# One planner run from a stored table of priorities, and PSUM matmuls tied in order

## The chip, the core and the metric

The kernel runs on one NeuronCore of a Trainium2 chip. The metric is the device time of one execution in microseconds (us), median over runs. The engines are TensorE (PE), ScalarE (ACT), VectorE (DVE), GpSimd (POOL) and SyncE (SP); SP issues all the DMAs of this kernel. Each engine works off its own queue in program order and waits on semaphores for the others.

## The reference

What is computed, cut to what matters (two batches, 8 heads, 768 positions, head size 64; then two feed-forward layers on 1536 tokens, width 512, hidden width 2048):

```python
q_bits = (q @ proj > 0); k_bits = (k @ proj > 0)
mask = q_bucket[:, :, :, None] == k_bucket[:, :, None, :]
scores = where(mask, q @ k.T / sqrt(64), -1e9)
attn = exp(scores - max); attn = attn / (sum(attn) + 1e-9)
x = (attn @ v) as tokens x 512
h = x @ w_in;  x = (h * sigmoid(h)) @ w_out
h = x @ w2_in; x = (h * clip(h + 3, 0, 6) / 6) @ w2_out
```

All inputs and outputs are float32. The kernel keeps the accuracy by splitting each operand into two float16 parts (high and low) and multiplying three of the four combinations.

## The kernel before

**The work.** Batch 0 has four head pairs, batch 1 four more. A pair is prepared (`Pair.prepare`, L715): q and k are loaded (L612), their squares summed on ACT (L382), scaled and split into halves (L388 on ACT, L394 on DVE or POOL), transposed by DMA (L652), hashed (products L665, sums L671, penalties L677), and transposed again with the penalties in the spare columns (L696). `Unit` (L723) then does one pair and one block of two query tiles, in four slots: scores (L749, L750), negated row maximum (L753 on DVE), scale and bias (L755, L758), exponential with row sum (L761 on ACT), and the product with v. In batch 0, blocks 0 and 1, this product is exact: PE transposes (L777), copies (L783) and float32 matmuls (L789). Elsewhere the exponentials are split in two float16 halves (L808 on ACT, L810 on POOL or DVE), transposed by DMA (L813) and multiplied (L803). `finish` (L818) divides and writes the block into X^T by another DMA transpose (L847).

The weights come in chunks (`Weight`, L403): load into one of three stage buffers `st` (L444 on SP), then L446 (ACT), L447 (POOL), L449 and L451 (DVE), square sums, and after all chunks of a group the splits (L388, L394). W1I and W1O are the weights of the first layer, W2I and W2O those of the second.

`mlp1` (L884) does the first layer for one block of 256 tokens: 16 hidden tiles (matmuls called at L876, activation L919, DVE product L921, split L388 and L394), then four output tiles of 48 matmuls each (L933). `mlp2` (L975) does the second layer for groups of 512 or 256 tokens: L876, L1008, L1012, L1014, L1015, L1016, L1021, results scaled (L1037) and stored (L1040).

**What sets the order.** Nothing is issued when this code is reached. Each step is an `op` (L215): one or more `ways` (engine, cost from the fixed formulas of class `Cost`, function), the cells that it reads and writes, and the `take` and `give` of a shared PSUM buffer. Dependences follow from the cells. A step such as L394, L755, L783, L810 or L1037 has two ways, and the planner picks the engine. There are 3171 steps. `Run` (L114) is a list scheduler: it keeps a model time for each engine, and picks again and again the step that can start earliest (`choose`, L190); the rank decides only between steps with the same start:

```python
key = (s, -self.ranks[i], sign * i, e)
```

`Run.start` (L170) also models the DMA queue and the SBUF port that POOL and some DVE steps share, and `Clock` (L81) a TensorE clock with two levels. `Plan.issue` (L255) takes the longest path behind each step (`paths`, L245) as the first ranks, runs the planner forward, runs it backward over the result, takes the ends of the backward run as the next ranks, and does so 24 times (`PASSES`). The best forward run by model time is issued, engine by engine, in its order and with its choice of ways (L264). `follows` (L861) links PE steps by a soft edge, used by `paths` alone.

**PSUM and order.** A group of matmuls that accumulates in one bank is cut into several PE steps: two for each hidden tile (L914 to L917), eight for each output tile of `mlp1` (L940 to L943), 16 for each output tile of `mlp2` (L1030 to L1032). The first matmul of a group carries `start=True`. Before the change no dependence orders the steps of one bank among each other.

Of the kernel before, what the change touches and what calls it, by code (L numbers as in the profile page):

```python
# [2 lines left out]

# [262 lines left out]

# [859 lines left out]
```

## Time and profile before

| | us |
|---|---|
| median of three runs | 746.33 |
| lowest and highest run | 745.91 to 746.54 |
| span of the profiled execution, first to last instruction | 745.7 |
| PE busy in the span | 689.2 |
| ACT busy | 513.1 |
| DVE busy | 507.3 |
| POOL busy | 182.5 |

The profile has no second time for its execution than the span, which ends 0.6 us below the median of the runs. Busy times are unions of the instructions' spans on an engine. A matmul in a stream is shown with its own latency, so the mean of one is longer than the distance between two.

### The profile page before, as it was taken

Reading aid. Unit: us, or ns where it says so; the run is one execution under the profiler, and the core shown is the slowest. Engines: PE = TensorE matmul, PEld = TensorE weight load, DVE = VectorE, ACT = ScalarE, POOL = GpSimd, SP = SyncE. Lnnn points to the kernel's source line nnn. Section 1 sums busy time; section 2 is a strip of 40 time slices with the busy share of each in tenths; the row PEclk is TensorE's granted clock in tenths of the full one; section 3 lists DMA queues with packets and bytes.
Section 4 is the critical chain, followed back from the end, with each engine's and each line's share of the span. In section 5 each row is a group of like instructions: output and inputs, shape, how many; then the busy total and the mean of one; then the engine's idle time right before and its main releaser. Section 6 shows DMA issues by size and latency. Waiting matters only on the chain.

```text
span 745.7 us, 15542 instructions
## 1 busy us (share of the span) xinstructions
PE 689.2 (92%) x6012; PEld 507.9 (68%) x6012; DVE 507.3 (68%) x1157; ACT 513.1 (69%) x1016; POOL 182.5 (24%) x174
## 2 busy tenths in 40 slices
PE   0499989669999999899999999999999999999997
PEld 0288878548778888788888888864445664444564
DVE  5898999899878987887795889843333443333343
ACT  7689999989989987898676888832324334233433
POOL 1011322243656675677422220000000000000000
PEclk9999999859999999999999999999999999999999
DMA  9999465586899999999746450000000000000100
GB/s 263 253 256 251 147 186 170 191 181 139 190 214 207 215 211 194 214 168 177 198 145 220 134 182 2 1 2 0 1 1 30 28 1 29 1 1 0 57 1 29
DMA packets 182474, 91.19 MB, mean 122 GB/s; under 512 B 164992, under 2 KB 172160, under 8 KB 182400
## 3 DMA queue, kind: packets, MB, share of 16 engines
q1 hardware_dynamic: 182400, 90.20, 50.2%
q8 instruction: 47, 0.77, 0.4%
q14 instruction: 27, 0.22, 0.1%
HBM read 44.57 MB, written 3.15 MB: 64 GB/s over the span
## 4 chain that ended last, share of the span: by engine, by line
PE 56%; DMA 13%; ACT 12%; DVE 10%; issue 5%; POOL 2%; SPq 2%; POOLq 0%; ACTq 0%; DVEq 0%
PE h L876 22%; PE s L1021 17%; PE h L933 9%; DMA T<-G 3%; DMA PT<-PN 3%; ACT e L761 3%; ACT sq L382 3%; PE o L789 2%; DVE nm L753 2%; DMA st<-in_moe_w_in_dram 2%; PE s L749 2%; PE s L750 2%; PE o L803 1%; PE h L777 1%; ACT PN L808 1%
## 5 line engine op out<-in xcount | busy, mean ns | idle before, releaser
L1021 PE MATMUL s<-y,G 128*128 128x512 f16 x576 | 134.6, 379 | 0.8 <-ACT w L1037 0.8
L933 PE MATMUL h<-G,w 128*128 128x256 f16 x1152 | 134.1, 273 | 0.1
L810 POOL TENSOR_TENSOR PN<-e,PN 128x768 f16<-128x768 f32 x64 | 107.8, 1687 | 73.5 <-ACT PN L808 55.3
L876 PEld LDWEIGHTS <-w 128*128 128x128 f16 x1152 | 112.0, 99 | 20.0 <-issue 2.7
L933 PEld LDWEIGHTS <-w 128*128 128x128 f16 x1152 | 110.7, 98 | 14.3 <-issue 0.5
L1008 ACT ACTIVATE g<-h,table 128x256 f32<-128x256 f32 x96 | 50.6, 561 | 88.0 <-PE h L876 87.9
L761 ACT ACTIVATE e<-s,nb,sc 128x768 f32<-128x768 f32 x96 | 96.3, 1003 | 3.9 <-DVE nb L758 2.3
L1021 PEld LDWEIGHTS <-G 128*128 128x128 f16 x576 | 56.2, 98 | 62.7 <-issue 1.1
L753 DVE TENSOR_REDUCE nm<-s 128x1 f32<-128x768 f32 x96 | 91.2, 951 | 11.1 <-PE s L750 10.4
L1012 DVE TENSOR_SCALAR g<-g 128x512 f32<-128x512 f32 (+1 forms) x64 | 23.1, 360 | 103.3 <-ACT g L1008 103.3
L876 PEld LDWEIGHTS <-T 128*128 128x128 f16 x576 | 56.4, 98 | 42.1
L447 POOL TENSOR_SCALAR st<-st 128x512 f32<-128x512 f32 x64 | 50.3, 787 | 140.3 <-ACT w L446 59.8
L749 PE MATMUL s<-T 128*128 128x384 f16 x192 | 65.3, 341 | 16.2 <-ACT e L761 16.0
L1015 ACT ACTIVATE G<-g 128x512 f16<-128x512 f32 (+1 forms) x64 | 33.4, 522 | 64.5 <-DVE g L1014 62.8
L876 PE MATMUL h<-X,w 128*128 128x256 f16 x576 | 71.8, 276 | 1.1 <-DVE g L921 1.1
L876 PE MATMUL h<-T,w 128*128 128x256 f16 x576 | 65.1, 272 | 2.5 <-DVE hx L366 1.0
L750 PE MATMUL s<-T 128*128 128x384 f16 x192 | 65.6, 342 | 1.0 <-DMA T<-N 0.8
L1016 DVE TENSOR_TENSOR G<-g,G 128x512 f16<-128x512 f32 (+1 forms) x64 | 35.7, 559 | 41.1 <-ACT G L1015 40.5
L808 ACT ACTIVATE PN<-e 128x768 f16<-128x768 f32 x61 | 51.1, 840 | 6.8 <-DMA PT<-PN 6.5
L876 PE MATMUL h<-X,T 128*128 128x512 f16 (+1 forms) x288 | 50.9, 326 | 0.0
L876 PE MATMUL h<-T,T 128*128 128x512 f16 (+1 forms) x288 | 50.7, 326 | 0.0
L789 PE MATMUL o<-w,PT 128*128 128x64 f32 x384 | 46.2, 271 | 0.2 <-DVE x L838 0.2
(123 smaller groups left out, 1106.4 us busy)
## 6 DMA issues: line engine op xcount, KB each, us to landing
st<-in_moe_w_in_dram SPq DMA_DIRECT2D x32, 512.0 KB, 4.5
st<-in_moe_w_out_dram SPq DMA_DIRECT2D x32, 512.0 KB, 3.5
qk<-in_v_dram SPq DMA_DIRECT2D x8, 384.0 KB, 4.0
out_dram<-w SPq DMA_DIRECT2D x12, 256.0 KB, 2.0
qk<-in_q_dram SPq DMA_DIRECT2D x6, 384.0 KB, 3.6
qk<-in_k_dram SPq DMA_DIRECT2D x6, 384.0 KB, 4.3
w<-in_v_dram SPq DMA_DIRECT2D x2, 768.0 KB, 9.5
T<-T SPq DMA_DIRECT2D x8, 192.0 KB, 3.2
```

What stands on the lines that cost most here:

```text
L447: op((POOL, Cost.pool_ts(512), lambda: nc.gpsimd.tensor_scalar(st.t[:, :, 1].bitcast(F32), st.t[:, :, 1].bitcast(F32), 0.0, 1.0, op0=ALU.m ...
L749: nc.tensor.matmul(o, t.t[:, 0, c, :], t.t[:, 1, ks, :], start=True, stop=False)
L750: nc.tensor.matmul(o, t.t[:, 2, c, :], t.t[:, 3, ks, :], start=False, stop=True)
L753: op((DVE, 0.865, lambda: nc.vector.tensor_reduce(nm.t, ps.t[:, :, :HS], op=ALU.max, axis=AX.XY, negate=True)), [(ps, 0)], [(nm, 0)])
L761: op((ACT, 0.97, lambda: nc.scalar.activation(e.t.rearrange("p (n c) -> p n c", n=2), ps.t[:, :, :HS], AF.Exp, bias=nb.t, scale=sc.t, accu ...
L789: nc.tensor.matmul(po(), pt.t[:, kt, :], vraw.t[:, v0 + a, kt * D : (kt + 1) * D], start=(kt == 0), stop=(kt == T - 1))
L808: op(ways((ACT, Cost.act(S), lambda: nc.scalar.activation(pn.t[:, 0], e.t, AF.Copy)), (DVE, 0.47, lambda: nc.vector.tensor_copy(pn.t[:, 0] ...
L810: op(ways((POOL, Cost.pool_tt(S), lambda: nc.gpsimd.tensor_tensor(pn.t[:, 1], e.t, pn.t[:, 0], op=ALU.subtract)), (DVE, Cost.tt(S), lambda ...
L876: nc.tensor.matmul(ph, W[f, wl, kt, :], XT[b].t[:, kt, ts, xl, :], start=(c == 0), stop=(c == 3 * NK - 1))
L933: nc.tensor.matmul(pf.t[:, :n], W1O[f, wl, slice(m * P, (m + 1) * P)], G.t[:, f, gl], start=(f == 0 and c == 0), stop=(f == NF - 1 and c = ...
L1008: nc.scalar.activation(g.t[:, cs], pf.t[:, cs], AF.Relu, bias=three, scale=a)
L1021: nc.tensor.matmul(acc[m // 2].t[:, m % 2, :DM], gs.t[:, f % 3, gl, m * P : (m + 1) * P], W2O[f, wl], start=(f == 0 and c == 0), stop=(f = ...
```

## The change

`PASSES`, `paths` and the alternation of forward and backward runs are removed. A string `RANKS` is added; unpacked it holds one whole number of 16 bits for each of the 3171 steps, and these are the ranks of a single forward run. `nearest` takes out every dependence that follows from others, before that run. Each PE step on a PSUM bank of the two layers writes a further cell, `(bank, "seq")`, so that the steps of one bank depend on each other in the order in which the code makes them. `Cost`, `Run`, the tiles, the buffers and every instruction's function stay.

```diff
-PASSES = 24
+RANKS = (
...
+)
...
-    def paths(self):
...
+    def ranks(self):
+
+        raw = zlib.decompress(base64.b85decode(RANKS))
+        n = len(raw) // 2
+        assert n == len(self.ops)
+        ranks = [0] * n
+        for i in range(n):
+            ranks[i] = (ranks[i - 1] * (i > 0) + raw[i] + 256 * raw[n + i]) & 0xFFFF
         return ranks
 
+    def nearest(self):
+
+        behind = [0] * len(self.ops)
+        for o in self.ops:
+            o.succ = []
+        for o in self.ops:
+            far = 0
+            for d in o.deps:
+                far |= behind[d.index]
+            behind[o.index] = far
+            for d in o.deps:
+                behind[o.index] |= 1 << d.index
+            o.deps = {d for d in o.deps if not far >> d.index & 1}
+            for d in o.deps:
+                d.succ.append(o)
+
     def issue(self):
 
-
-        best, ranks = None, self.paths()
-        for _ in range(PASSES):
-            run = Run(self.ops, ranks)
-            if best is None or run.time < best.time:
-                best = run
-            ranks = Run(self.ops, run.ends, run.engines).ends
+        self.nearest()
+        best = Run(self.ops, self.ranks())
         for i in best.order:
             next(w[2] for w in self.ops[i].ways if w[0] == best.engines[i])()
...
-                               xt_cells(b, tiles) + W1I.cells(f + i), [(pf, i, h)]))
+                               xt_cells(b, tiles) + W1I.cells(f + i), [(pf, i, h), (pf, "seq")]))
...
-                           gc + W1O.cells(f) + W1O.cells(f + 1), [(pf, f)]))
+                           gc + W1O.cells(f) + W1O.cells(f + 1), [(pf, f), (pf, "seq")]))
...
-                           xt_cells(b, tiles) + W2I.cells(f), [cells[h]]))
+                           xt_cells(b, tiles) + W2I.cells(f), [cells[h], (pf, "seq")]))
...
-                               [(gs, (f - 1) % 3, 0), (gs, (f - 1) % 3, 1)] + W2O.cells(f - 1), [(acc[m // 2], m, f)]))
+                               [(gs, (f - 1) % 3, 0), (gs, (f - 1) % 3, 1)] + W2O.cells(f - 1), [(acc[m // 2], m, f), (acc[m // 2], m, "seq")]))
```

## Rows read from the trace of the kernel before

**Rows 1.** The page: span, then busy time, share and instructions of each engine.

```profile
span 745.7 us, 15542 instructions
PE 689.2 (92%) x6012; PEld 507.9 (68%) x6012; DVE 507.3 (68%) x1157; ACT 513.1 (69%) x1016; POOL 182.5 (24%) x174
```

**Rows 2.** Busy time by stretch: length, engines, granted clock, DMA share, GB/s.

```profile
0.00:41.75 41.75, 14.22 (x100) 10.04 (x101) 29.33 (x85) 28.80 (x52) 4.85 (x15) 1.00 1.01 254
41.75:144.15 102.40, 95.34 (x827) 85.03 (x826) 95.47 (x238) 100.05 (x217) 25.49 (x35) 1.00 0.71 199
144.15:164.63 20.48, 10.86 (x54) 6.42 (x54) 17.78 (x43) 18.48 (x37) 8.65 (x8) 0.50 0.71 180
164.63:340.00 175.37, 170.47 (x2222) 143.11 (x2221) 150.25 (x355) 158.68 (x310) 105.00 (x76) 1.00 0.98 195
340.00:420.00 80.00, 77.12 (x812) 67.76 (x810) 58.31 (x121) 59.67 (x125) 30.89 (x34) 1.00 0.65 179
420.00:740.00 320.00, 319.86 (x2000) 195.19 (x1999) 156.11 (x319) 146.04 (x281) 7.62 (x9) 1.00 0.07 24
```

**Rows 3.** The chain that ended last, in order of time: start, us, what.

```profile
503.74 2.59 PE s L1021 x12
...
510.21 2.59 PE h L876 x12
```

**Rows 4.** PE's timeline around 150 us: start, us, what, [idle before].

```profile
139.83 1.47 PE L876 MATMUL h<-X,w 128*128 128x256 f16 x12
147.27 0.48 PE L749 MATMUL s<-T 128*128 128x384 f16 x1 [5.96 <-ACT e L761]
...
153.57 0.48 PE L749 MATMUL s<-T 128*128 128x384 f16 x1 [0.47 <-ACT e L761]
...
158.49 0.48 PE L749 MATMUL s<-T 128*128 128x384 f16 x1 [3.48 <-ACT e L761]
...
160.83 1.44 PE L876 MATMUL h<-X,w 128*128 128x256 f16 x6 [0.40 <-DVE g L921]
```

**Rows 5.** SP's queue at the start: start, us, what.

```profile
0.81 0.46 SPq L612 DMA_DIRECT2D qk<-in_q_dram  x1
12.86 4.75 SPq L652 DMA_TRANSPOSE T<-N  x1
...
18.85 4.82 SPq L652 DMA_TRANSPOSE T<-G  x1
24.93 3.21 SPq L696 DMA_TRANSPOSE T<-N  x1
```

**Rows 6.** Waits within 164.63 to 340 us, PE: us in total, times, longest.

```profile
PE s L749 <- ACT e L761: 2.2, 3, 1.2
PE o L803 <- DMA PT<-PN: 0.9, 2, 0.7
```

**Rows 7.** Waits of SP's queue in the first 380 us.

```profile
SPq L444 <- DVE w L451: 52.2, 22, 4.9
SPq L813 <- POOL PN L810: 26.9, 19, 5.3
```

**Rows 8.** Line L813, the transpose of the exponentials: ns min/median/max, first and last start.

```profile
L813 SPq DMA_TRANSPOSE PT<-PN x64: 1286/1429/2657, 150.3 to 355.4; - x64
DMA to landing us min/median/max: 3.2/3.7/5.4
```

**Rows 9.** Lines L810 (POOL), L394 and L449 (DVE): ns min/median/max, first and last start.

```profile
L810 POOL TENSOR_TENSOR PN<-e,PN x64: 1635/1645/2206, 148.6 to 353.7; 128x768 f16<-128x768 f32 x64
L394 DVE SCALAR_TENSOR_TENSOR G<-g,table,G x48: 720/746/2134, 138.2 to 474.0; 128x512 f16<-128x512 f32 x48
L449 DVE SCALAR_TENSOR_TENSOR w<-w,st x32: 676/683/2173, 17.6 to 148.6; 128x512 int32<-128x512 int32 x32
```

**Rows 10.** The last PE instructions, their result and its store.

```profile
741.30 1.92 SPq L1040 DMA_DIRECT2D out_dram<-w  x2
741.33 0.81 PE L1021 MATMUL s<-y,G 128*128 128x512 f16 x3 [0.78 <-ACT w L1037]
742.18 0.69 ACT L1037 ACTIVATE w<-s,table 128x512 f32<-128x512 f32 x1 [0.90 <-PE s L1021]
```

More of the change, by code (lines that the diff above doesn't have):

```diff
@@ L1 @@
+import base64
 import math
+import zlib
 from contextlib import ExitStack
@@ L24 @@
 STEP_IN = 1
-PASSES = 24
+RANKS = (
+    'c-mc82_O~S7oU0ZvVWEmC9+khq~cR4qLQUhDj`z#EhSq*ktMtA6p17W$yO<}SSouWOOl<eh0vS%zc+X0J>S1F=H9vYp7T5BcYf!#U3_Ff^c=IE`Pdi9js=amPpg>N*trImSo=233(Rtst<4cW6LXxI'
+    'qm-q{j*ImL%g+(*MaeO-p&q{B4{S%i*Lo)Ra?5dS%l-kcOL)waQNMr6Y;q6##K{CX=?y!OV(D12#4d4lQ3a3iX0lUK-edoil%IECN#P}<GTj#aA0~PVoKtI@x8IHR5~<NT#b#)CiEX_Ph1c|zNcWEy'
+    '&mzc$!5&$<z6VBw<(_FsM%Tzz=pITgf10AKdW~;!YiKLiieFhzubud3qvQcWr_WXb+TmskdJXIp&PNN<)q5_cb*4O8cXj=#g_5As+0cYTCww0)SxU?YtFb=Vbj$H}nA=7FJRKw6a-Dz0Qn<L00*BiZ'
+    '&-Q9~{I1pLeqoh?IDVF^s_~C*-o4vef|9b2?8N@iCL`lsZMcZe7n7+<r8n&NEWX9GR-De4za^C{G87a&XYbOcq~ZXl%t^NY{`zERz4=n}u$5Wo2Ue@cBGTfbwf$yNZwogL>ZQ!fJJ#eB8MSt9?k(OX'
+    '>3Z>-(fJoazq&NaGM)sW<N-Z%&*x_;u>pRE3&~?In{AJeYfcD+20q%mWsddNI>prePn{DQ{+f$Vo_cwNZRJQ%ho^FZS>D6JhfjF-j})XvkqkY|+r!*BBI9!A`wIk<$ZSa=2HLWgQ8EL33*UO~M2DBI'
+    'KGkF|RevwKuG8POy;<)2s0`9DCEccOr`7dvPCi&1W|e(==YXceK@-g=-`lE{SEYS@*0s7V-GAev#%>_3c~3oqM}%`BNL{TwprUBilto8=;JC)PbD`-G@6vrNc^XT<T>Ox4dZIm3aypZO8V?nwcvibP'
+    '@vY%5Qxfj#o4UC^EqZ8Yt{$79h=Y#8=DV811!d1$M>aBvcE(4x&Bx6Dnv(dS{*I;MWO3%1gDY3DTp*Dgt8^ZhTHiyJ8r&@sc%pstl2T<Qzbf!=RSXrXyJvgt&(1F^)+9($3YFad?5zn@6MdY!s8L(@'
+    'hA;cV5L4HOf0>z$J74ngW@fRCT{)LnPKpQ#MP`aZE(Tab{3?^rG9~xC-u=>KL(OM9OGh2)M3o@jQ@b|v1^r6CATOFPeBoBxp0gX;zE<BB@UJ<YSSq$?<DBj$t<+M*F_4_){&8C5yai9tM7qTRy|Zba'
+    'E~$&=(M*Be(w&W!-=$4V-ilpluOxlFQz4Vc-SV)kKIv+(N|8#fn?t?oK#AJ0>T4bNgIoPkXr@8dk)ouB@ca?WcVoZQbK_`%(6?N6k1g*{3Orx&IV$+)bT4U4oGHcB+-Gh6!rD<s6)oYpr>_SoGk%p@'
+    'tXUQ1#<zw;`@|>JCk7)wbMyYu&*<6m*z9_n(^I4_+TX{1Q%;?rYF(<gK&R!Pp<nroeMnBJwZxD0tr8tV@le|NeR|*ONsdanXu-_RPFHBYHm9N0HZ4QQJnd1pji8SMr;*`>q&8&ETJ@t!j$!Y%xRh?s'
+    'oioPPp%Z`gcWLofG>ylXygl^&d+2<(*Yzv0hEm%qpG}6}<%slng4#BB_<e?@N?)XPe-jg3)Y6Q7|LNid)Aa0+`ofYhj-MkU3PX)nCgMyRCmQT^PG(lT%E%n+Z8C@v`A5t1UGu|_aRSzD(Zz;Uma(?M'
+    'o8LW`7m&X!Ki^?6p{LkCacGfy6Jk+#v<~{}(cwv&?)Q#l+HMrLwAIgZ+;yJ~dOGn<U1iPQEoDY??1;yaz66upQ2s<n;7-=12Dibm)hEuS?cdeGGUAjsKlHAvHa~bxX;<J0$&1Ijauv(kS(@grUUGIw'
+    '3h9F!{D<ECYhL$->&yvP=KB$9@q5H69m-na5_u_G()POS`*{bIA?F1KPm64bzYmS66?H8%2K<pPPBI#o-P!h$ZRjw`MI+6BbL>aHY@yK0!7@VfCCMgd5WyhR?Z<A~tvgbf_+<6RU4I2nmRDzIE3HYf'
+    'G(Nsob(g8qlfHG+RwC?T&kR-!7Yq4B-C9j)*!H|w=E3ZO&=tEttI)3-cYN>lgtxsAj9Rd7-7!P))hQxn=?)HG4Q7IBQMJ2|6#KWCC~asQ`FcHM^=HG#SF4vU^EA{8oLAHi$UCdToPNl}w5k5*HJM<`'
+    'mkQsRY88ugd3}~5g0GY#6>Dn`564CHm5fwut`v=VU3&Xw+WqpVoE2Z*DOniL$<3ppobI_gW0?xV(X*Z_J@>x7Gkr-rxJ9B(CHRY8t*Y_XK*O=SM*~icobzzmXO<ha$2!*2xbMV*1xx#2bd6VgV7XR('
+    'nQzlSx{)V^Bd=7=<|%G>ZA8?Bg}EgR-p`$d?x&69&j@<0v~o_@*A8`!qYONVe^;w98|HPaSoEFtiCukACaG=dPm8;poygvhe*$J~O-)}-gxuWdb!dP4v4x7Exme~MugRK9b@GL*$$!#x8WR-bSnpkm'
+    'SylIBw~yBIdhaB^z3Rd?Ua9xZKPMinTX`YZrhjGf*6pK~str}w!Xu@thncTsC7-FdskwVW)lyDuG<`gl>^;|XILW*64Ec9%&RDnqnN@6#oO2ydj5HPAL_DaSxWt(?)4Mx<Nd9^RQ*svn)vTkim-v#I'
+    'lbl+>-0BSlg4wT!#zW0XF*~!*FO-g5b80VU=UR~Rb#Tz-)X(gHB(`4r+Nbtv0j|^b8E+hRBsh%a=%p~38*D;vU+S2&@4w|<UBvM^zDwqfv1*o5GdX6p_zNRjZCSG$C60G2-=7JLlc`eM;V*4UKFB(D'
+    'd9w9j(KBXc{gz#Nbv2g^9&Hf_+bQi7;OBlYBYiw%mfy6FwWa&vB|qIEXh-$-o1=y^r<-M(c%45;2&?r(9R6gUW9jrM*(*4zbn*O@baR<ZpGH1<L*kGsSL3kX%l<8Ei>w@{uI!M=_Zs}JQKa)XBO+{M'
+    'AKZDX$6ot*TE5^ngQboi+m(;Te!O9^@@>OgkH*Co<Ll~XS0bb#-;rBnF)1st%kpx2j(!yr-^72`f836x#?w5~^nni2)e$2%&LSshcRXhLeoMeTrAwh7x9a#przJVcr3@8&*l!*kZIt)g_tcpEG|#{d'
+    '-6~7@_MYTaW<}P?-(glCWm3JA*)!j$4-8#?ZD#oK>Ug#J+Rp>Z9$ew9vUlZq*ebniPjO`E3q$tgLe*K88#fO4?2SDmvpew1_d_-6y}mh3*`pUC5{m?!KDf%ciapEhu@kyrEu-T4h54)E!5e3fbJ$E2'
+    'Fvneq&kQW&=C`+<dM~TXZ)0Q~#C&m7W?a$u<cw>hVc2O7o4(6vlFJ$e-Py=**=x_4?M&a}tjy9?_}uGS_xWp%mK&7Lj+;G|SlUdk30@d8;f)WztUqb5)0S$k@at8x{%(<1dZIgiulC_j@OH{Lp?c+@'
+    '@QbnYdB?>wwStc)%igr=v*y?0vwM3+@_v#n?}y!{E?MC}4g0QMXIES>ui0+Yd-FF(MOE$J4$X?qzMOuI&DL_4MaEVPe|7MiSM^STT(o3WVzsy37co^{%4c^gxT2r$nz+@zal*4L=1Oj+!yn1G4II%!'
+    '_G+V=FX9JIp3{7i$P^)6b1`=h`-e5hrp5h!zd88ot7+V+^iLxV%4KYk$2azzytOtA&TgN#aTlE-{|fBnHh%vQm2q`e8tqR!AGzpWz0hhFWA`B2uB7$P-B;quImRuc3RP$AuFA>!Z|4^D4_ALCI?gp+'
+    'X>bFMr+6y3E2esLj`~z)+};pVj_{V;5}WOLU!^a1sFTBm<#$ww;mei0MY7s^Hjhhe?Do!>%{$kVHY%xIzTP@-@=G%BWXDk{ll-WG(cA-v-bNKhJ)QHl=Mj!d$+Ovbs^pW)dtFKYQ6tN-;z3UfM2QdS'
+    '?A;YmEs<6nVUgyyKS-)MExmie_Q)VR&!3PS)XsW%Li~tOfnrapn}q*S=LfT7o{a59njNhiTdGM13^cUsi-pPx=6~6DmihFbo&52ZJT72;k-Wdt==>DdnwF5Mtz=Gp3yMU%#<RbBe}yM}AI-^eudTYd'
+    '6zTBIKb>qPAGc$^&dAn!OvY|nILzf`ep;?t-^!sc8x!pxd)=Ept!>dN?YzTboep^f75h-Tv0qZ{w(u&ol$}M;?5?$3MZ%L~%rX%xPmOb`+pTkJTIIC)-@}CpTaPIBE?jh(4^8g#u##D_TH+_gHaDNu'
+    'U9{&7Dsd62wfM<irPBis3^tu!iVb$NY4kMupuW`jIIF#;I&W2p!2^kzF2QxJK|Wl)liaP|FC1*yj}`83|97wC(M3L~AJeRe_$QR@7ylT{%)EjFonwVi2!c=)rT#`~uV6qMK?sb!fC24^fL9bOMTs3?'
+    '0260WM+i#7-{|{MYzeY#gndI`d<+q`P+$odr#V3#5N3#NU=4KzN`1f(1%~lC;%w><jNtAe*m-oAR5u_7005EZJc?TbYiL-(P8d6j`h*db;VVKQrv5?@5@8RZhhPMc7VRrGz$^h9v@pP!E$Rn^IwD~!'
+    ';lH>q2p(?)hfIY>qy$At6cXe8FAW~mEd-)Yg7DCs!Cc1ifVhDJ@bu8*hPgqTLog?)pJ56;g&?K0cpyv&ksu0&1qQwW7cr1{E+MLI3>HG70EAeE5d?+-Zg4J*A2ce^LPm8BqPh&NVB`isK?p(-%plT+'
+    '=LgRl)g_3)M<F3FP8+Zj!8`=vpuUh8X{R}g;;!Sz(`-WwTGM#}l8Muw<~oiWWmE&<7C}w?3F1hhk&5m(#31N$vO;*cV4OD;63Qqb8bpvEJUB$$!9N&ekh+mXCp9gq7#pwz;4T8rg4`h(xpBq=^k5O~'
+    'L81nqg5d;3L}whmR+d4bokt<j+=M`&F>?s@1!F1#1H*XSA%dLLFDocmnUJV|Y55^x&SLz+yeE!Fa23HYQh%^mfa1UskNJ+Xg*J`*48RhGakw~CGWAITA4ur3d6W@il#x?V8UO?WG5y76Fji1^P?JNe'
+    '5eNo#MLm#$Sp(m(oFZ5*5RB>&@Dm20XyOKVjnx(m>Ys)NCenoBZ@?Oag_X*BLJn~)0V+g29sWy;9|bQo1nkDj48b#p6+Y$~iC`0!C~EC96qE)7*ArT$;1Y`B(E>-~N&;wyfR8AsNeJj21*Ypgl~6EI'
+    'Y$Wgs1A(NuL&7|w#RE?sP1Il*BL>xV7}GdFBP`eu=`U53Q0#mfMyyP!Q<$O>(ZUizfkD(@OaU-3K>iRw9ta3D1OyP&8(0fA!2}knF%(3Mb|R)}2*wR;DNIW^R$mB4DWU~{asf&~hzV8g5NNqdU~-5R'
+    'Fr!&Q^d3iJJSb^gvT*sK7vX=zhrW|gPnslxS(vUJKuxf&23i}i4ujPQU2{=9O`wth285wngoG?}3p2`u(uI|=1jVC_rvpzXHpb8s<&2343>q<rF~$NE$Qa|YLimH7LwF4n!b;aG2*Se#T%)p@kOc$;'
+    'iRerugxCo(MPnL*=ME*3NgxGHo^YQwWWognQ)5v3;6%`xXeEbn1ZNt64mu7aCdAbQM+w9NzjZC^g+K*y^tcMp^^b%ybR5R>g>#%Z7^@MWJs4b=f;TtfJ_OVN=oAWi-m=RbjNedj5)&;4PwRgKcNxtY'
+    '7;r77PoQ*05iOR%V~CMy;*y3%9zvJ3X}q1#FOSP^4a5$-TcR+7(Fh@9%lbCmL0ncLqMI$lfa1LvrDuvTi>o`(#bx(Vl(-9`I7^Y`LJQ&LN05?eV<^P9m@l)pd<6aH%7Oa@GY9|*7yAGEHB3K=euYPt'
+    'r-$JZew`&Q&h#bdf3H6D{~`Qerm27a2RgoWlK'
+)
```

5 lines of the change are left out of this document (removed).

## The prediction

> **What bounds the kernel now.** I read the page's busy shares first: PE is busy 92% of the span, no other engine over 69% [rows 1]. That average hides stages, so I cut the span where the granted clock changes and where the work changes [rows 2], and the reader should compare, in each row, PE's busy time with the row's length. From 420 to 740 us PE is busy 319.86 of 320 us, and the chain of waits there is PE alone: twelve matmuls of 512 columns every 2.59 us, 216 ns each, without a gap [rows 3]. What comes before decides only when this block begins; no order makes it shorter. Up to 420 us PE is idle for 27.5 us (0 to 41.75), 7.1 us (to 144.15), 9.6 us (to 164.63), 4.9 us (to 340) and 2.9 us (to 420), each the row's length less PE's busy time [rows 2].
>
> The third row is the one that stands out: the granted clock is 0.50, the lower of its two levels (1.2 GHz against 2.4), for 20.48 us, after PE had stood idle. PE's timeline shows the hole: a batch of L876 ends near 141.3 us, and the next matmul starts at 147.27 us; PE then does single slots of scores with waits of up to 3.48 us on ACT's exponential [rows 4]. At the lower clock six matmuls take 1.44 us where twelve took 1.47 us [rows 4]. So the 10.86 us of PE work in this row are worth about 5.4 us at full clock, and the row holds 20.48 - 5.4 = 15 us in which PE gets nothing done. ACT is busy 18.48 and DVE 17.78 of these 20.48 us, and ACT 100.05 of the 102.40 us before [rows 2]: there the weights of the first layer are finished beside the first units of batch 1. These are engines at their limit, which an order can only relieve by moving work to where they have room: ACT is idle 13.0 us before 41.75, 16.7 us between 164.63 and 340, 20.3 us between 340 and 420 [rows 2].
>
> **The change part by part.** The kernel's steps, tiles, buffers and instruction forms stay; what changes is the order on every engine's queue, SP's and POOL's included, and the choice between two ways for steps that have them.
>
> *The tie of PSUM steps* adds no instruction. In the order that the kernel before issues, the steps of every bank of the two layers already stand in the order that the tie demands (136 groups, listed from the code), so against that order it moves nothing; it only fences the new one in. Zero, and its cover is that PE's queue is in order anyway.
>
> *The removal of dependences that follow from others* acts in the planner alone; a step waits for the same steps through the nearer ones. Zero.
>
> *The table.* Unpacked it is a permutation of 0 to 3170. It gives many steps a higher rank than steps they depend on, so it isn't a length of path; its coarse order is that of the present kernel: the same stages after each other. Among details, the 124 steps of W1O stand on average at place 652 of the table, against 690 in the order issued now, while the preparation of batch 1's first pair stands at 853 against 843: the first layer's second weight is put forward against batch 1. That is the right direction for the hole at 141 to 165 us. Rank decides only between steps that can start at the same model time, so a change of place acts where several steps queue for one engine: ACT and DVE up to 340 us.
>
> No row shows what the new order costs; I bound it by stretch, by the idle time there.
>
> 1. 0 to 41.75 us: the path is loads, square sums, splits, and four transposes in SP's queue, the first issued at 12.86 and the third not before 24.93 us [rows 5]. PE's 27.5 us of idle time are mostly this path, which stays. A transpose sent before the other pair's would save its 4.82 us of issue; one sent late would cost as much or less. I take 2 us saved, bounds 6 saved to 3 lost.
> 2. 41.75 to 144.15: PE idle 7.1, but ACT only 2.35 us [rows 2]. I take 1, bounds 0 to 2.3, since every step of the units in this row but the copies has ACT in its chain.
> 3. 144.15 to 164.63: up to 15 us. I take 8, half: the hole is made by work on ACT and DVE that must still be done, but can follow the first layer's start, where ACT has its 16.7 us. Bounds 0 and 15.
> 4. 164.63 to 340: PE idle 4.9; PE's own waits in the view of waits are 2.2 us on exponentials and 0.9 us on transposes [rows 6]. I take 2, bounds 0 and 4.9. If work moved out of term 3 fills ACT here, this is what turns late next.
> 5. 340 to 420: PE idle 2.9. I take 2, bounds 0 and 2.9.
> 6. From 420 us: PE idle 0.14 us. Zero. The end, last matmuls at 741.33 us, one scaling and two stores [rows 10], stays: zero.
>
> Sum: 2 + 1 + 8 + 2 + 2 = 15 us of 745.7 us. The profiled span lies 0.6 us below the median of the runs, so the same 15 us off 746.3 give **731 us**. The upper bounds add to 6 + 2.3 + 15 + 4.9 + 2.9 = 31 us (715 us), the lower ones to a loss of 3 (749 us).
>
> **A rule weighed against the rows.** Where a DVE and a POOL instruction meet, the rows show it: L394 has a median of 746 ns and a maximum of 2134, L449 683 and 2173, while POOL's L810 stays between 1635 and 2206 ns [rows 9]. So some DVE instruction now and then waits up to 1.4 us for POOL, and few do, as the medians are at the minimum. The Trainium skill, page "SBUF — State Buffer", section "Who interferes with whom", says that a DVE instruction with two SBUF inputs and a GpSimd instruction that reads SBUF exclude each other for the whole instruction. The maxima agree with it. It would speak against this change, if the new order brought such pairs together more often; that is the last rival.
>
> **The rivals.**
>
> *Less than half of it (13%).* ACT and DVE are full from 41.75 to 164.63 us, the hole stays for want of their time, and only its edges move. Then terms 2, 4 and 5 remain in part, some 4 us: 742 us. For it: the busy sums of the third row. Against: the idle ACT time right after.
>
> *All of it (10%).* The hole goes wholly and the start is shortened: 715 to 721 us.
>
> *No change (6%).* The rank only breaks ties; if steps rarely compete, the order comes out nearly as now: 746 us. Against: the hole, where steps of three kinds compete for ACT.
>
> *Slower, by SP's queue (9%).* SP issues in order. A weight load (L444) waits for its stage buffer to be freed by DVE's L451: 22 such waits in the first 380 us, 52.2 us in all, so 2.4 us each [rows 7]. Now little stands behind them. If the table puts loads of weights ahead of transposes that are ready, each holds up a slot of batch 1: 64 transposes L813 of 1.43 us issue and 3.7 us to landing between 150 and 355 us [rows 8], one slot every 3.2 us, with three buffers of cover. From six exposed waits (6 x 2.4 = 14 us) the gain is gone; eleven cost 26 us, and with the 15 won elsewhere the time is **757 us**. Against it: SP's waits on L444 are there already, and PE still waits only 0.9 us for these transposes [rows 6].
>
> *Slower, by the port (4%).* Between 164.63 and 340 DVE is idle 25.1 us [rows 2]. If the new choice of ways and order makes DVE wait 1.4 us behind half of the 64 subtractions of L810, that is 45 us, 20 more than the idle time; less the 15 won, 751 us. It decides from 25.1 / 1.4 = 18 blocked instructions on. By the page's rule this takes no more than overlap; by the medians of rows 9 it is rare.
>
> **How the numbers follow.** The forecast (721 to 741 us) has 58%. With "all of it" and "less than half" faster comes to 0.58 + 0.10 + 0.13 = 0.81, same is 0.06, slower 0.09 + 0.04 = 0.13. "Same" means within 0.2%, 1.5 us, about what a measurement of this kernel can tell from no change. The range goes from 716 us, the sum of the upper bounds within a microsecond, to 749 us, the loss of the lower bounds; it leaves out most of the two slower cases and the edge of the fast one, some 15%.
>
> **What would show it.** In the changed profile the row of clocks should have no slice at half clock between 140 and 170 us, and PE's timeline no hole of 6 us behind the first batch of L876; the block of L876 and L1021 without gaps should have the same length, 216 ns for a matmul of 512 columns, and begin some 15 us earlier. PE's busy sum should fall by about 5 us (the half clock) and its idle time by about 10. ACT's idle time before 340 us, now 34 us, should shrink to about 20. The prediction is wrong if the hole is still there, or if a new one opens further back: then the half clock would show again, or PE's waits on L813's transposes (the queue) or stretched L394 and L449 (the port) would have grown to many microseconds.

## The result, and the profile after

The change takes **753.43 us**, the median of four runs (750.80 to 754.10), against 746.12 us for the kernel before (four runs, 744.94 to 746.54): a ratio of 1.0087, 95% interval 1.0062 to 1.0113. A later repeat gave 753.70 against 747.88 us, 1.0104 [1.0065, 1.0144]. It is slower by some 7 us, where 15 us less were forecast, and outside the range of 716 to 749 us. Times are medians; a ratio with its interval is worked out from all executions and need not be the quotient of two medians. One execution further below (763.31 us, the splice of the table's front), over 1.5% slower than the fastest of its kernel, is left out of that kernel's median and ratio.

The page of the changed kernel: span, busy sums, then 40 slices with the tenths in which PE was busy, and the granted clock. (In its line numbers everything of the kernel before stands 52 lines further down: L749 is L801, L761 L813, L813 L865, L876 L928, L1021 L1073, L444 L496.)

```profile
span 749.1 us, 15563 instructions
...
PE 685.6 (92%) x6012; PEld 504.8 (67%) x6012; DVE 503.3 (67%) x1162; ACT 511.8 (68%) x1014; POOL 178.3 (24%) x171
...
PE   0499988967999999999999999999999999999997
...
PEclk9999999999999999999999999999999999999999
```

No slice shows a fallen clock, and PE's busy sum is 3.6 us smaller than in [rows 1]. Yet the span is 3.4 us longer, so PE stands idle 7.0 us more. The stretches of [rows 2], cut at the same times (length; busy PE, PEld, DVE, ACT, POOL; granted clock; DMA share; GB/s):

```profile
0.00:41.75 41.75, 14.26 (x104) 9.57 (x105) 29.93 (x87) 29.67 (x53) 4.43 (x15) 1.00 0.95 263
41.75:144.15 102.40, 93.45 (x806) 83.52 (x805) 95.03 (x235) 98.75 (x212) 24.98 (x34) 1.00 0.71 198
144.15:164.63 20.48, 14.17 (x115) 11.01 (x114) 19.91 (x46) 20.48 (x37) 7.52 (x6) 1.00 0.69 184
164.63:340.00 175.37, 162.56 (x2144) 135.63 (x2144) 144.21 (x357) 155.18 (x309) 103.69 (x74) 1.00 1.01 193
340.00:420.00 80.00, 78.13 (x836) 68.96 (x835) 60.02 (x126) 61.39 (x125) 28.75 (x32) 1.00 0.68 175
420.00:740.00 320.00, 318.31 (x1996) 194.29 (x1995) 152.61 (x312) 144.07 (x279) 8.94 (x11) 1.00 0.07 24
...
80.00:140.00 60.00, 52.19 (x434) 46.47 (x434) 57.95 (x140) 59.32 (x126) 15.12 (x21) 1.00 0.58 180
140.00:160.00 20.00, 16.47 (x141) 13.56 (x140) 19.39 (x46) 19.86 (x37) 6.00 (x7) 1.00 0.65 201
160.00:200.00 40.00, 31.49 (x393) 25.22 (x392) 34.40 (x79) 36.75 (x75) 20.80 (x15) 1.00 0.91 171
200.00:340.00 140.00, 132.93 (x1767) 111.58 (x1765) 114.23 (x286) 123.06 (x243) 85.82 (x61) 1.00 1.04 200
```

and the kernel before, in the same view, cut finer than in [rows 2]:

```profile
80.00:140.00 60.00, 56.31 (x479) 50.76 (x479) 57.62 (x137) 59.76 (x125) 16.18 (x21) 1.00 0.54 173
140.00:160.00 20.00, 7.93 (x33) 4.13 (x31) 16.56 (x40) 18.00 (x36) 8.02 (x7) 0.60 0.80 218
160.00:200.00 40.00, 38.63 (x429) 32.88 (x430) 38.16 (x87) 38.37 (x77) 16.09 (x12) 0.94 0.68 151
200.00:340.00 140.00, 136.07 (x1827) 113.55 (x1826) 116.53 (x281) 124.94 (x245) 90.59 (x66) 1.00 1.05 203
```

Read PE's number in each pair. The hole and the half clock are gone: 16.47 us at full clock stand where 7.93 us at 0.60 stood. But PE has 4.1 us less before it (52.19 against 56.31) and 7.1 us less right behind it (31.49 against 38.63, a little of the latter at half clock). From 200 to 340 it loses 3.1 us more. ACT is busy in all of 144.15 to 164.63. From 160 to 200 us neither ACT (36.75 of 40 us) nor DVE (34.40) is full, and yet PE waits there for 8.1 us in all, against 1.2 us before, mostly for their results (us in all, times, longest):

```profile
PE s L801 <- ACT e L813: 3.3, 4, 1.3
PE p_hash L717 <- DVE hs L723: 1.6, 1, 1.6
PE h L928 <- DVE g L973: 1.6, 1, 1.6
```

Busy time at two clocks can't be added, so I counted for both kernels how much PE work is done by a given time, each matmul taken at the distance two of its kind have in a full stream (216 ns for 512 columns, 162 for 384, 109 for 256). Differences to the kernel before, in us (positive is ahead; they shift by up to 0.4 us with how the small matmuls are counted):

```
by (us)              40    140    160    200    340    420    740
before (done)       5.8   99.9  104.1  140.1  273.7  349.8  669.8
the change         +0.3   -5.0   +6.5   +0.1   -2.5   -1.3   -3.5
the change, again  +0.1   -6.4   +5.0   -0.4   -2.2   -2.2   -5.8
```

So in the profiled execution the front is a draw at 200 us, 2.6 us are lost by 340, 1.2 won by 420, and 2.2 lost from there, where PE had no gap (1.6 of them as waits, below). Of the 7 us between the medians the profiled executions show 3.4. How much of the rest is the clock of single executions is weighed in the last section.

PE's timeline around the old hole [rows 4] (start, us, what, idle before):

```profile
138.82 7.48 PE L928 MATMUL h<-X,w 128*128 128x256 f16 x67
149.83 2.78 PE L928 MATMUL h<-X,w 128*128 128x256 f16 x24
...
153.49 0.32 PE L801 MATMUL s<-T 128*128 128x384 f16 x1 [0.87 <-ACT e L813]
...
162.14 0.32 PE L801 MATMUL s<-T 128*128 128x384 f16 x1 [1.17 <-ACT e L813]
...
164.56 1.69 PE L928 MATMUL h<-X,w 128*128 128x256 f16 x14 [1.60 <-DVE g L973]
```

The table has put matmuls of the first layer where PE waited 5.96 us; waits of 0.9 to 1.6 us on ACT and DVE remain.

### The profile page after: what moved, and what is told of

Its sections match the earlier page's. It is cut to its first block, busy times and chain, and to the rows that moved or that the text cites. A ratio compares the mean times of both kernels' runs of the same rounds, so it can differ in the third digit from the quotient of the medians.

```text
span 749.1 us, 15563 instructions
## 1 busy us (share of the span) xinstructions
PE 685.6 (92%) x6012; PEld 504.8 (67%) x6012; DVE 503.3 (67%) x1162; ACT 511.8 (68%) x1014; POOL 178.3 (24%) x171
## 4 chain that ended last, share of the span: by engine, by line
PE 61%; DVE 13%; ACT 12%; DMA 9%; issue 4%; POOL 1%; SPq 1%; DVEq 0%; ACTq 0%; POOLq 0%
PE h L928 25%; PE s L1073 16%; PE h L985 11%; DMA PT<-PN 4%; ACT e L813 3%; DMA st<-in_moe_w_in_dram 3%; DVE nm L805 2%; ACT sq L434 2%; PE s L801 2%; PE s L802 2%; PE o L841 2%; PE o L855 2%; DVE w L446 1%; ACT PN L860 1%; PE h L829 1%
## 5 line engine op out<-in xcount | busy, mean ns | idle before, releaser
L1073 PE MATMUL s<-y,G 128*128 128x512 f16 x576 | 134.9, 379 | 2.3 <-ACT w L1089 2.3
L862 POOL TENSOR_TENSOR PN<-e,PN 128x768 f16<-128x768 f32 x64 | 107.2, 1679 | 74.6 <-ACT PN L860 46.6
L928 PEld LDWEIGHTS <-w 128*128 128x128 f16 x1152 | 111.3, 99 | 18.2 <-issue 3.2
L813 ACT ACTIVATE e<-s,nb,sc 128x768 f32<-128x768 f32 x96 | 94.7, 988 | 7.5 <-DVE nb L810 6.1
L1073 PEld LDWEIGHTS <-G 128*128 128x128 f16 x576 | 56.3, 98 | 64.4 <-issue 3.2
L928 PEld LDWEIGHTS <-T 128*128 128x128 f16 x576 | 55.9, 98 | 42.2 <-DVE g L1066 3.2
L499 POOL TENSOR_SCALAR st<-st 128x512 f32<-128x512 f32 x64 | 47.4, 743 | 143.9 <-ACT w L498 57.3
L801 PE MATMUL s<-T 128*128 128x384 f16 x192 | 64.0, 334 | 14.9 <-ACT e L813 14.7
L928 PE MATMUL h<-X,w 128*128 128x256 f16 x576 | 69.4, 272 | 3.1 <-DVE g L973 2.8
L928 PE MATMUL h<-T,w 128*128 128x256 f16 x576 | 64.2, 273 | 0.3 <-DVE g L973 0.2
L802 PE MATMUL s<-T 128*128 128x384 f16 x192 | 64.0, 334 | 0.1
L860 ACT ACTIVATE PN<-e 128x768 f16<-128x768 f32 x59 | 49.4, 840 | 5.8 <-DMA PT<-PN 5.5
L928 PE MATMUL h<-T,T 128*128 128x512 f16 (+1 forms) x288 | 50.9, 326 | 0.0
L928 PE MATMUL h<-X,T 128*128 128x512 f16 (+1 forms) x288 | 50.7, 326 | 0.1
L855 PE MATMUL o<-V,PT 128*128 128x64 f16 x1152 | 43.1, 193 | 5.9 <-DMA PT<-PN 4.6
```

Of the source, the lines that this page charges most:

```text
L499: op((POOL, Cost.pool_ts(512), lambda: nc.gpsimd.tensor_scalar(st.t[:, :, 1].bitcast(F32), st.t[:, :, 1].bitcast(F32), 0.0, 1.0, op0=ALU.m ...
L801: nc.tensor.matmul(o, t.t[:, 0, c, :], t.t[:, 1, ks, :], start=True, stop=False)
L802: nc.tensor.matmul(o, t.t[:, 2, c, :], t.t[:, 3, ks, :], start=False, stop=True)
L813: op((ACT, 0.97, lambda: nc.scalar.activation(e.t.rearrange("p (n c) -> p n c", n=2), ps.t[:, :, :HS], AF.Exp, bias=nb.t, scale=sc.t, accu ...
L855: nc.tensor.matmul(po(), pt.t[:, pl, kt, :], V.t[:, a, vh, kt * D : (kt + 1) * D], start=(i == 0 and kt == 0), stop=(i == 2 and kt == T - 1),)
L860: op(ways((ACT, Cost.act(S), lambda: nc.scalar.activation(pn.t[:, 0], e.t, AF.Copy)), (DVE, 0.47, lambda: nc.vector.tensor_copy(pn.t[:, 0] ...
```

## The experiments

**Which part of the change acts.** The order that the planner issues can be worked out from the code. The old planner with the tie, with `nearest`, or with both issues on every engine the same order as before; the whole effect is the table's. By the planner's own model, which is no time of the chip, the old order takes 726.6 and the table's 723.9 us. The tie matters to the table, though: without it the planner makes of the same ranks an order that it times at 780.7 us. That order was not run.

**Where it acts.** A splice issues each stretch in one or the other order (`alternate` is the removed 24 runs to and fro). Where the order changes is the splice's seam: the second order finds engines and buffers there in a state for which it was not planned. A step belongs to the stretch in which the old order has it (982 steps: about 197 us; 2581: about 527 us).

```diff
-        self.nearest()
-        best = Run(self.ops, self.ranks())
-        for i in best.order:
-            next(w[2] for w in self.ops[i].ways if w[0] == best.engines[i])()
+        old = self.alternate()
+        self.nearest()
+        new = Run(self.ops, self.ranks())
+        place = {i: n for n, i in enumerate(old.order)}
+        low = 0
+        for high, run in ((982, new), (len(old.order), old)):
+            for i in run.order:
+                if low <= place[i] < high:
+                    next(w[2] for w in self.ops[i].ways if w[0] == run.engines[i])()
+            low = high
```

*The table's front, then the old order:*

> The first 982 steps of the old plan (about 197 us of the profile of before) are issued in the table's order, all later ones in the old order. Theory (the table moves the hole at 141 to 165 us but ACT and DVE had to do the same work, so the front is worth nothing, and the loss comes from later stretches): 745 to 748 us, no change against before. Rival (the exact units, where the changed profile fell 5 us of PE work behind by 140 us, are what loses): 750 to 752 us. My old forecast (the hole is worth 8 us): 738 us.

752.93 against 748.01 us: 1.0065 [1.0043, 1.0087]. The theory missed, and so did the old forecast; the rival's 750 to 752 us is nearest. Its profiled execution, the fastest of six (750.26 us), is nearly level at 200 us by the count (-0.8) and ends 2.6 us behind. So what this profile loses, it loses mostly behind the seam, in steps that stand in the old order.

*The old front, then the table's* (`(982, old), (len(old.order), new)`):

> The mirror image: the first 982 steps of the old plan in the old order, all later ones in the table's order. Theory (the loss comes after 200 us): 750 to 754 us, as slow as the change. Rival (the front loses): 745 to 747 us.

758.08 us: 1.0132 [1.0110, 1.0155], slower than either expectation.

*The table's order up to 527 us* (`(2581, new), (len(old.order), old)`):

> Table's order up to step 2581 of the old plan (about 527 us), then the old order. Theory (some 2.4 us of the loss are the gaps of 0.78 us at the changes of output block in the second layer, the rest lies before): 749 to 751.5 us. Rival (the second layer is filled by PE alone and costs nothing in either order): 753 us, the same as the change.

753.85 us: 1.0080 [1.0056, 1.0104], the rival's number.

*The table's tail alone* (`(2581, old), (len(old.order), new)`):

> Old order up to step 2581, then the table's. Theory (2.4 us lost at the changes of output block): 748 to 749 us. Rival (nothing is lost in the second layer): 746 us.

751.07 us: 1.0048 [1.0030, 1.0066], slower than either expectation.

*The middle alone*, steps 1126 to 1957 of the old order, which lie between about 220 and 374 us (`(1126, old), (1958, new), (len(old.order), old)`), beside the change once more:

> Old order for the first 1126 steps of the old plan (about 220 us), the table's up to step 1958 (about 374 us), the old one again. Theory (the table loses 2 to 4 us in the middle, where the DMA transposes set the pace): 1 to 6 us slower than before, 749 to 754 us; DMA waits of PE above those of before. Rival (the middle is as good in either order, the loss is in the front and the tail): within 1.5 us of before.

> The changed kernel once more, timed beside the kernel before on the chip of the other runs of this call, so that they have it as a measure: 0.7 to 1.1% above before, 751 to 756 us.

754.64 against 747.88 us: 1.0085 [1.0061, 1.0109], at the slow edge of the theory; the change again 1.0104, as expected.

Every splice is slower than the kernel before; none found a part of the table that pays. But front, middle and tail add to 0.65 + 0.85 + 0.48 = 2.0%, twice the whole, and do not even cover all of it, which points at the seams. The planner's model prices the seams with the rest: 0.3 us for the table's front, 2.2 us for the old front before the table's order, 1.2 us for the tail, 1.9 us for the middle, where the chip lost 4.9, 10.1, 3.1 and 6.8 us. How much of each is the stretch and how much the seam is not shown. By the count of PE's work the middle falls back from -1.5 us at 200 to -6.6 at 340; PE's waits in that splice, 164.63 to 340 us (us in all, times, longest):

```profile
PE o L881 <- DMA PT<-PN: 3.4, 5, 1.0
PE s L827 <- ACT e L839: 3.1, 6, 1.1
```

and in the change, 200 to 340 us:

```profile
PE o L855 <- DMA PT<-PN: 3.0, 3, 1.2
PE s L801 <- ACT e L813: 2.5, 2, 1.3
PE o L855 <- DVE x L890: 1.0, 1, 1.0
```

against 0.9 and 2.2 us before [rows 6].

**The tail, read off.** Three profiles, PE's waits on L1089 or what answers to it, from the middle on: first the change, then the table's tail alone, then the table's order up to 527 us.

```profile
PE s L1073 <- ACT w L1089: 2.3, 3, 0.8
```
```profile
PE s L1099 <- ACT w L1115: 2.3, 3, 0.8
```
```profile
PE s L1099 <- ACT w L1115: 0.8, 1, 0.8
```

PE's timeline of the change where an output block ends, and then of the kernel before:

```profile
618.00 1.46 PE L928 MATMUL h<-T,y 128*128 128x512 f16 x6
619.29 1.46 PE L1073 MATMUL s<-y,G 128*128 128x512 f16 x6
621.53 1.46 PE L1073 MATMUL s<-y,G 128*128 128x512 f16 x6 [0.78 <-ACT w L1089]
```
```profile
617.77 1.46 PE L1021 MATMUL s<-y,G 128*128 128x512 f16 x6
619.07 2.75 PE L876 MATMUL h<-T,y 128*128 128x512 f16 x12
621.66 0.59 PE L1021 MATMUL s<-y,G 128*128 128x512 f16 x2
```

The next block's first product needs the PSUM banks that L1089 scales out. The old order covers that with a hidden step of 2.59 us (L876); the table has none there, and PE waits 0.78 us at 621.53 and again at 702.13 us. The third of the 2.3 us is the one at the end, which the kernel before has too [rows 10], and with the old tail that one alone is left. The profile of the tail alone has one wait more, 1.07 us at 531.01 us on DVE's g, just behind its seam. Two waits are 1.56 us, as much as the last row of the windows shows (318.31 against 319.86 us of 320). In the planner's model that wait is 0.0 in both orders. Here the table ends work just in time by the model, and the chip is a little later.

**Would more margin in the plan pay?** 0.1 us added to each hand-over between engines in the planner's costs:

```diff
+    LATENCY = tuple(tuple(t + 0.1 * (a != b) for b, t in enumerate(row)) for a, row in enumerate(LATENCY))
```

> The planner of before (24 runs to and fro, no table), but with every hand-over between two engines planned 0.1 us longer. Theory (the table's order loses because it leaves PE too little margin between the planned readiness of its operands and its turn, and more margin pays): 741 to 746 us, no slower than before. Rival (hand-overs take on the chip what the planner assumes, and margin is waste): 750 to 753 us.

> The table's ranks with the tie, but hand-overs planned 0.1 us longer. If the ranks describe a good order as such: 750 to 755 us. If they fit only the exact numbers of the cost model for which they were found, so that the planner falls into other ties: over 770 us.

With the old planner 751.77 against 747.46 us, 1.0068 [1.0050, 1.0086]: 4.3 us longer, and the model's plan had grown by 5.6 (726.6 to 732.2). With the table's ranks a single run of 802.91 us, 55.5 above; its plan is 782.3, 55.7 above. So 0.1 us of margin at every hand-over does not pay (the rival's number); margin at chosen hand-overs was not tried. The model follows the chip within 1.3 us for these two, and is wrong by about 10 for the table (-2.7 in the model, +7.3 measured). And the table holds only for costs close to those in the kernel: with hand-overs 0.1 us longer the same ranks are 7% slower.

**What sets the pace of the front?** Each suspect is made lighter, in the old order and in the table's. These kernels leave out part of the computation, as their expectations say. First ACT, 16 square sums of the first layer's weights over 64 columns in place of 1024:

```diff
...
-                    lambda: raw.t[:, i - 1 : i + 1, :].rearrange("p a b -> p (a b)"),
+                    (lambda: raw.t[:, i, :64]) if self.name[:2] == "W1" else
+                    (lambda: raw.t[:, i - 1 : i + 1, :].rearrange("p a b -> p (a b)")),
...
```

> The old order, with 16 square sums of the first layer's weights on ScalarE over 64 elements instead of 1024 (0.95 us each by the trace, so about 13 us of ScalarE work less before 190 us; the sums, and so the scales of these weights, are other numbers). Theory (up to 200 us ScalarE and VectorE are at their limit, so the hole of PE is their work and only moves): 5 to 13 us faster, 733 to 742 us. Rival (the hole is a matter of order; ScalarE has room): less than 3 us, 743 to 746 us.

> The table's order with the same 16 square sums cut down. Theory (engines at their limit in either order): 5 to 13 us below the change's 753 us, so 740 to 748 us. Rival: less than 3 us below it.

Old order 745.15 against 747.46 us, 0.9977 [0.9958, 0.9997]; table's order 1.0098 [1.0074, 1.0122], no gain: the rival's numbers in both. Then DVE, the bit merges of the same weights over 64 of 512 columns:

```diff
+            w = 64 if self.name[:2] == "W1" else 512
...
-                bits(), st.t[:, :, 0], 29, bits(), op0=ALU.logical_shift_right, op1=ALU.bitwise_or), True), [cell, sc], [cell])
+                bits()[:, :w], st.t[:, :w, 0], 29, bits()[:, :w], op0=ALU.logical_shift_right, op1=ALU.bitwise_or), True), [cell, sc], [cell])
```

> The old order, with VectorE's second bit merge of the first layer's weights (32 instructions, 0.69 us each) over 64 elements of 512: some 17 us less VectorE work before 155 us (the lowest three bits of most of these weights are left out). With ScalarE relieved by 13 us nearly nothing was gained, and VectorE is busy 29.0 of 30 us from 110 to 140 us. Theory (VectorE sets the pace of the front): 5 to 13 us faster, 734 to 742 us. Rival (no single engine does; the in-order queues do, whatever one engine is spared): less than 3 us.

> The table's order with the same. Theory (VectorE sets the pace of the front, where it is busy 29.5 of 30 and 24.2 of 25 us): 5 to 13 us below the change, 740 to 748 us. Rival: less than 3 us below it, 750 us or more.

0.9994 [0.9978, 1.0010] and 1.0120 [1.0077, 1.0164]: nothing either. Both together:

> The old order with both reliefs of the front together: ScalarE's square sums of the first layer's weights over 64 elements and VectorE's second bit merge over 64. Theory (the two engines set the pace of the front in turn, so that one alone gains nothing): 5 us faster or more, 742 us or less, with PE ahead of before by that much at 200 us. Rival (the front hangs on something else, or what it gains is lost again where the DMA transposes set the pace): less than 3 us faster in time.

> The table's order with both reliefs. Theory: 5 us or more below the change. Rival: less than 3 us below it.

742.61 against 747.88 us, 0.9931 [0.9908, 0.9954], 5.3 us, the theory's gain; table's order 749.57, 1.0029 [1.0012, 1.0046], 4.1 us below the change beside it, between theory and rival. The windows from 80 to 140 us, with ACT light, then with both:

```profile
80.00:140.00 60.00, 56.10 (x466) 50.59 (x466) 56.57 (x135) 53.72 (x128) 17.79 (x21) 0.97 0.55 167
```
```profile
80.00:140.00 60.00, 57.55 (x492) 52.12 (x492) 52.29 (x147) 56.29 (x134) 15.43 (x23) 1.00 0.60 180
```

With ACT light, ACT has 6 us of room (53.72 of 60), DVE has 3.4 and PE is busy no longer than before (56.10 against 56.31). With room on both PE gets 1.2 us more in this window. The profile with ACT light is among the slowest of its ten executions (748.06 us, median 745.15) and its clock fell once more than before, for 3.4 us at 122 us, so the times and the count weigh more than its row. By the count at 200 us PE is 0.5 us behind the kernel before with ACT light, 1.0 us ahead with DVE light and 3.8 us ahead with both; in the table's order 0.2 us ahead, 3.0 us behind and 5.6 us ahead. In the old order the two single gains, 2.3 and 0.8 us, together come too near the 5.3 us of both to tell a sum from more than a sum. In the table's order the singles gain nothing, and both together lie clear below them (1.0029 against 1.0098 and 1.0120). So in the table's order the front is held by both engines at once, and in the old order the runs agree with that. The hole itself stays in the old order even with both light: the granted clock from 144.15 to 164.63 us is 0.62. What else holds it is not shown.

**And the middle?** The transposes of the exponentials (L813, L865) move half of their data, the values read the first half twice:

```diff
-                out=pt.t.rearrange("p h t c -> p (h t) c"), in_=pn.t.rearrange("p h c -> p (h c)"))),
+                out=pt.t[:, 0], in_=pn.t[:, 0])),
...
-                            po(), pt.t[:, pl, kt, :], V.t[:, a, vh, kt * D : (kt + 1) * D],
+                            po(), pt.t[:, 0, kt, :], V.t[:, a, vh, kt * D : (kt + 1) * D],
```

> The old order, with the DMA transposes of the exponentials (64 of them) for the high halves alone; the values products read these in place of the low ones (the low part of the product is wrong by that). The DMA engines are busy without a break from 200 to 340 us (share 1.05). Theory (the middle of the kernel runs at the pace of the DMA transposes): 3 to 6 us faster, up to PE's own limit there (136 of 140 us busy). Rival (PE sets the pace): within 2 us of before.

> The table's order with the same. Theory (the table loses its 3 to 4 us in the middle to transposes that come late): 6 to 9 us below the change, within 3 us of the old order with the same edit before the tail's 2.4 us. Rival (it loses them to order on ScalarE and VectorE): as far above the old order with this edit as the change is above the old one, 6 to 7 us.

Old order 743.31 against 748.40 us, 0.9939 [0.9917, 0.9960]: 5.1 us. Table's order 747.74, 0.9996 [0.9977, 1.0015], where the change stood at 1.0087 and 1.0104 beside other executions of the kernel before: 7 to 8 us. The windows 200 to 340 us, old order, then the table's:

```profile
200.00:340.00 140.00, 138.90 (x1874) 117.26 (x1872) 120.69 (x289) 128.53 (x255) 94.61 (x69) 1.00 0.73 139
```
```profile
200.00:340.00 140.00, 136.43 (x1844) 115.58 (x1842) 119.54 (x292) 126.78 (x253) 89.36 (x63) 1.00 0.74 138
```

The DMA share falls from 1.05 and 1.04 to 0.73 and 0.74, and PE gains 2.8 and 3.5 us; ACT does more too, 128.53 against 124.94 us. So the transposes hold this stretch in both orders, and rather by the DMA engines than by SP: SP's time for one falls only from 1.43 to 1.22 us.

But the table's own loss does not go with them. PE's busy time differs between the two orders by 3.1 us with whole transposes (136.07 against 132.93) and still by 2.5 us with half ones (138.90 against 136.43). PE's waits from 164.63 to 340 us with half transposes, in the old order, then in the table's:

```profile
PE p_tot L358 <- ACT sq L382: 1.3, 1, 1.3
PE s L749 <- ACT e L761: 0.5, 1, 0.5
```
```profile
PE s L801 <- ACT e L813: 4.1, 5, 1.3
PE p_hash L717 <- DVE hs L723: 1.6, 1, 1.6
PE h L928 <- DVE g L973: 1.6, 1, 1.6
PE o L855 <- DVE x L890: 1.0, 1, 1.0
```

No wait for a transpose is left in either, and in the table's order the waits for ACT and DVE stand as in the change (4.7, 1.6, 1.6 and 1.0 us there). In time the two light kernels lie 4.4 us apart, which fits the theory's numbers and not the rival's 6 to 7; some 2 us of it are the tail's. The rows speak for the rival's reason, order on ACT and DVE. So late transposes alone do not make the table's loss here. No splice or variant that keeps the computation was faster than the kernel before.

## Why the prediction was wrong

**Right:** the tie and `nearest` cost nothing against the old order. The clock stays full between 140 and 170 us in the profile, the hole of 6 us is gone, a matmul of 512 columns keeps its 216 ns, and PE's busy sum fell by 3.6 us (about 5 forecast). **Wrong:** ACT's idle time before 340 us, which was to fall from 34 to 20 us, is 36 us (340 less ACT's 29.67, 98.75, 20.48 and 155.18). The hole was closed with time taken from its neighbours. Two readings of the prediction were wrong too. The units around the hole are not batch 1's but the third block of batch 0: the first pair of batch 1 is only loaded at 146 us. And places in the table are not places in the order that the planner makes of it. Worked out from the code, the steps of W1O stand at 691 on average in the issued order, against 690 before, and the first pair of batch 1 at 827 against 843: batch 1 was put forward, not W1O. On the chip the 16 loads of W1O are issued from 92.9 to 143.7 us (94.0 to 139.3 before).

- *Term 3, 8 us.* This step failed. Its mechanism was seen: between 140 and 160 us the change wins 11.5 us of PE work. But the term asked where the hole's work goes and answered "where ACT has its 16.7 us" behind 164.63, without pricing what PE loses meanwhile: 5.0 us before and 6.4 us right after, so at 200 us terms 1 to 3 together had brought 0.1 us in place of 11. ACT is busy 181.1 us of the first 200 before and 181.0 after. The sentence ahead of the sum had it: engines at their limit are relieved only by moving work to where there is room. Up to 140 us there was none: relief of ACT alone won 2.3 us or nothing, of DVE alone nothing clear of noise, of both 4 to 5. Behind 160 us ACT and DVE had some room, and PE waited for them all the same, 7.0 of the 8.1 us; which steps came too late there, and why, stays open.
- *Terms 1 and 2, 3 us.* Failed. +0.3 us at 40 us in place of 2, and then the loss of 5 us in place of 1 us won. In the planner's order the exact units of batch 0's second block start 1 to 3 us later than before and the values of batch 1 earlier (their fourth load is issued at 120.6 us against 140.0 on the chip). That these stood in the units' way is argued and not shown.
- *Term 4, 2 us.* Failed. It counted PE's idle 4.9 us as time to be won. The DMA share of [rows 2], 0.98 in that row (1.05 from 200 us on), was printed and not read. With half of the transposes' bytes the stretch ran faster in both orders, so there was little for an order to win. From 200 us on it lost 2.6 us in the profiled change and 5.1 in the splice of the middle. Late transposes are part of what PE waits for then, but the gap between the orders stays at 2.5 of 3.1 us without them; the term's own warning, that work moved out of the hole turns ACT's exponentials late next, fits the waits that are left. What makes them late is not shown.
- *Term 5, 2 us.* 1.2 us won, about right.
- *Term 6, zero.* Failed. That no order makes the block shorter is true, and the step took it for "the order doesn't matter there". It can make the block longer: two waits of 0.78 us at changes of block, 1.6 us. The tail alone cost 0.48% (3.1 us between the medians): 1.6 us are these two waits, 1.07 us the wait behind the seam, the rest stays open.

Of the rivals, "less than half" had the reason that held for the front (both engines full), though not its 742 us. **The port** is out: POOL's busy sum and DVE's are smaller than in [rows 1]. DVE instructions that take over 150 ns more than the median of their kind number 35 in either trace, and what they take more sums to 16.3 us in the change against 20.9 us before. **SP's queue** is not wholly excluded. The waits of SP's queue in the first 380 us, against 52.2 and 26.9 us in [rows 7]:

```profile
SPq L496 <- DVE w L503: 60.8, 26, 7.7
SPq L865 <- POOL PN L862: 37.5, 30, 2.6
```

and lines of the change to set against [rows 8, 9]:

```profile
L865 SPq DMA_TRANSPOSE PT<-PN x64: 1273/1422/2790, 156.3 to 358.0; - x64
DMA to landing us min/median/max: 3.2/3.7/6.3
...
L446 DVE SCALAR_TENSOR_TENSOR G<-g,table,G x48: 724/746/1160, 140.2 to 474.9; 128x512 f16<-128x512 f32 x48
...
L501 DVE SCALAR_TENSOR_TENSOR w<-w,st x32: 669/683/1200, 6.7 to 150.3; 128x512 int32<-128x512 int32 x32
```

There are four more waits for stage buffers (8.6 us) and eleven more for POOL. The slowest transpose lands in 6.3 us against 5.4, and PE waits for them 3 to 4 us against 0.9. That is the rival's direction at a small part of its price (14 us from six waits). No run here changes the queue's order alone; where transposes no longer make PE wait, most of the table's loss in this stretch stays.

The table's plan is the shorter one by the model, and it has less slack. In the two plans I counted the PE steps whose operands are ready less than 0.3 us before PE's turn: from 200 to 340 us 35 in the table's and 14 in the old order, from 480 to 740 us 46 against 6. Waits that are 0.0 in the plan can then show on the chip. For the tail that was shown; for the middle it is argued.

The Trainium skill, page "Perfetto Trace Analysis", section "Optimization Strategy", says that a kernel can have several regimes, with another engine most contended in each, and that interleaving them may help. The rows agree on the first part: ACT and DVE from 80 to 140 us (59.76 and 57.62 of 60 us), the DMA engines from 200 to 340 (share 1.05), PE from 420 (319.86 of 320 us). For the second no run here shows a gain; the table's form of it moved the loss.

## What to carry to other kernels

When a hole is to be filled by a new order, price the neighbours from which the work is taken: here two engines were full beside the hole, and it only moved. Where two engines are full, a test that lightens one of them can show nothing though both matter. Read the DMA share beside the engines in every stretch, and ask of a stretch that is full already not only what the order could win but what it could lose. A schedule that is a few microseconds better in a model may have paid for it with slack. A gain of 0.4% in the model is below the error that the chip showed here (10 us of 746). And read an order where it is issued: a table of priorities does not yet say what comes first.
